# Batch 0's states fetched first, expert products begun during attention 1, and the side work of an expert stream dealt into other slots

## The chip, the core and the metric

The kernel runs on one core of one Trainium2 chip. The metric is device time in microseconds (us) of one execution; the time before is the median of three runs. The profile and its trace come from one further execution. Engines: PE (TensorE, matrix products; PEld is its weight load), DVE (VectorE), ACT (ScalarE), POOL (GpSimd) and SP (SyncE, which here only issues DMAs and reads expert numbers into registers).

## What is computed

A block of cross attention between tokens and a few state rows, then a mixture of experts with one expert per token:

```python
B, H, S, Ns, D = (8, 8, 512, 32, 64)
scores = scale * x @ state^T;  a  = softmax(scores);   xread = a @ state
scores2 = scale * state @ x^T; a2 = softmax(scores2);  sread = a2 @ x
x = concat([xread, sread], axis=2), heads joined      # 4352 rows of 512
logits = x @ w_gate                                    # 8 experts
e = argmax(logits); g = softmax(logits)[e]
out = g * (relu(x @ w1[e]) @ w2[e])                    # w1 512x1024, w2 1024x512
```

All of it is float32.

## The kernel before

**Token rows.** Of each batch the kernel finds the expert that most of its 512 tokens chose, and runs the whole batch through that expert. `load_w1(b, e)` and `load_w2(b, e)` fetch 2 MB each (w1 has one buffer, w2 two); `states_w1` multiplies the batch's states into w1 (tile G, through PSUM tile pG), `up` makes the hidden layer from the attention weights and G (PSUM tile ph, relu by ACT into hT), `down` the result (PSUM tile py, scaled by ACT into y and stored by ACT's DMA queue). The few token rows that chose otherwise are counted at the end (`left`) and redone in a branch.

**State rows.** The 256 rows of `sread` go to DRAM (`write_rows`), are read back, routed (`logits_s`), sorted by expert (`sort_states`) and run in `rounds`: three rounds of 128 rows, in each four groups of 32 rows with an expert of their own. A round streams 16 tiles of 1 MB (tile s, four DMAs of 256 KB each, three buffers for w1 and three for w2) through SP's queue: four steps of `round_up` (PSUM pgh), relu, transposes (`round_h`, PSUM pth), four steps of two `round_down` (PSUM pgy).

**Attention.** `front(b)`: DVE transposes x (xt) and the states (stT), PE makes the scores of both directions in the PSUM tile pa, DVE transposes them (sx) and takes maxima (mx, nm), ACT the exponentials (sx, and a for the second direction). `back(b)`: `turn_read` transposes the softmax (aT), `logits_x`, `route` and `choose` give the batch's expert number eb, `write_rows` transposes a (a2T) and makes the state rows.

**What sets the order.** Every engine runs its instructions in the order in which the program was written (class `InOrder`). `front`, `back`, `logits_s`, `sort_states` and `rounds` are generators: each `yield` ends a piece. `up` and `down` call `insert` twelve times for a batch, at every fourth product of 512 columns; each call advances the generator `others` by one piece, so that 96 slots of expert products take up the other work. `run(...)` advances a `front` and a `back` side by side, and a slot passes empty where both have ended. Fronts 0 to 2 and backs 0 and 1 lie ahead of the first slot, with DVE in POOL's place for two passes over sx (`early`).

**DMAs.** Those from SP and ACT share eight completion semaphores in turn, so that one may have to wait for an earlier one to land before it is issued; a DMA that waits holds up what stands behind it on the engine that issues it.

Of the kernel before, what the change touches and what calls it, by code (L numbers as in the profile page):

```python
# [20 lines left out]
def kernel(  # L21
# [70 lines left out]
    def load_x(b):  # L92
        x_nat[b] = att.tile([128, H, NC, D], FP32, tag="x", bufs=2, name="x_nat")
        for h in (slice(0, 4), slice(4, 8)):
            sp.dma_start(out=x_nat[b][:, h].rearrange("p h c d -> p h (c d)"),
                         in_=x[b, h].rearrange("h (p c) d -> p h (c d)", c=NC))
# [4 lines left out]
    def load_states(b0, b1):  # L101
        rows = state[b0:b1].rearrange("b h n d -> n (b h) d")
        for i in range(4):
            to = st4[ts(i, 32), b0 * H:b1 * H]
            if i % 2 == 0:
                act.dma_start(out=to, in_=rows)
            else:
                for u in range(2):
                    act.dma_start(out=to[:, :, ts(u, 32)], in_=rows[:, :, ts(1 - u, 32)])

    load_x(0)
    load_states(0, 1)
    load_x(1)


# [37 lines left out]
    wg = const.tile([128, NDC, E], FP32)  # L153
    act.dma_start(out=wg[:], in_=moe_w_gate.rearrange("(c p) e -> p c e", p=128))

# [12 lines left out]
    eb_f = const.tile([128, B, 1], FP32)  # L168
# [14 lines left out]
    load_states(1, B)  # L183
# [4 lines left out]
    blank = att.tile([128, XW], I32)  # L188
# [10 lines left out]
    def front(b, early):  # L199

        xt = att.tile([128, H, NC, 2, 32], FP32, tag="xt", name="xt")
        flat = "p h c d -> p (h c d)"
        for h in (slice(0, 4), slice(4, 8)):
            if h.start == 4:
                dve.transpose(stT[:, b].rearrange("p h u n -> p (h u n)"),
                              st4[:, ts(b, H)].rearrange("p h d -> p (h d)"))
            dve.transpose(xt[:, h].rearrange("p h c u t -> p (h c u t)"), x_nat[b][:, h].rearrange(flat))
            yield
# [13 lines left out]
        act.copy(gst[:, b, :, 0:E], pa[:, 2:4, 1, 0:E])  # L222
# [9 lines left out]
        if early:  # L232
            act.activation(sx[:], sx[:], AF.Exp, bias=0.0, scale=SCALE)
# [4 lines left out]
        yield  # L238
# [6 lines left out]
        if not early:  # L245
            act.activation(sx[:], sx[:], AF.Exp, bias=0.0, scale=SCALE)
            yield
# [5 lines left out]
        dve.tensor_scalar(s2[:], s2[:], 1e-9, None, ALU.add)  # L253
        dve.reciprocal(s2[:], s2[:])
# [3 lines left out]
    def write_rows(b):  # L258
# [7 lines left out]
        yield  # L266
# [6 lines left out]
        xs = att.tile([128, 2, D], FP32, tag="xs", bufs=2, name="xs")  # L273
# [4 lines left out]
        if b + 2 < B:  # L278
            load_x(b + 2)
# [4 lines left out]
    def logits_x(b):  # L284
# [5 lines left out]
        dve.transpose(lg[:, ts(b, NC)].rearrange("p c e -> p (c e)"), pl)  # L290

    def back(b, early):

        if early:
            turn_read(b)
            logits_x(b)
            route(lg[:, ts(b, NC), 0:E], b * NC, NC)
            choose(b, 1)
            yield
            yield from write_rows(b)  # L300
            yield
        else:
            w = write_rows(b)
            next(w)
            yield
            turn_read(b)
            for _ in w:
                pass
            yield
            logits_x(b)  # L310
            b0, nb = {B - 3: (0, 0), B - 2: (0, 0), B - 1: (B - 3, 3)}.get(b, (b, 1))
            if nb:
                route(lg[:, b0 * NC:(b0 + nb) * NC, 0:E], b0 * NC, nb * NC)
                yield
                choose(b0, nb)
            yield

    def logits_s():
# [3 lines left out]
        for _ in range(3):  # L322
            yield
        sT = att.tile([128, NST, NDC, 128], FP32, tag="sT", name="sT")
# [11 lines left out]
        route(lgs[:], NX, NST)  # L336
        yield

    def route(lg, u0, U):
# [16 lines left out]
        dve.tensor_reduce(gw[:, r, 0], ex[:], AX.X, ALU.add)  # L356
        dve.tensor_scalar(gw[:, r], gw[:, r], 1e-9, None, ALU.add)
        dve.reciprocal(gw[:, r], gw[:, r])

    def choose(b0, nb):  # L360

        pr = pa[:, 2, 1, 128:128 + nb * E].rearrange("p (b e) -> p b e", b=nb)
        ohb = oh[:, 0:NX].rearrange("p (b c) e -> p b c e", c=NC)
        for c in range(NC):
            pe.matmul(pr, lhsT=ones_b[:], rhs=ohb[:, ds(b0, nb), c, :],
                             start=(c == 0), stop=(c == NC - 1), skip_group_check=True)
        r = ds(b0, nb)
        dve.tensor_copy(out=cnt[:, r], in_=pr)
        dve.tensor_reduce(cmx[:, r, 0], cnt[:, r], AX.X, ALU.max)
        cc = att.tile([128, nb, E], FP32, tag="c_cc", bufs=1, name="c_cc")  # L370
        dve.tensor_tensor(cc[:], cnt[:, r], cmx[:, r].to_broadcast([128, nb, E]), ALU.is_ge)
        dve.tensor_tensor(cc[:], cc[:], rev8[:].unsqueeze(1).to_broadcast([128, nb, E]), ALU.mult)
        dve.tensor_reduce(eb_f[:, r, 0], cc[:], AX.X, ALU.max)
        dve.tensor_scalar(eb_f[:, r], eb_f[:, r], -1.0, float(E), ALU.mult, ALU.add)
        dve.tensor_copy(out=eb[:, r], in_=eb_f[:, r, 0])
# [62 lines left out]
    def down(hT, w2t, store, insert=None):  # L438
        for c in range(NC):
# [7 lines left out]
            if insert:  # L447
                insert()

# [99 lines left out]
    def round_x(r):  # L549
        pt = late["ps_t"].tile([128, NDC, 128], FP32, tag="t", name="ptx")  # L550
# [14 lines left out]
    def round_h(r):  # L565
        h = late["sst"].tile([128, F], FP32, tag="sh", bufs=1, name="sh")
        for half in range(2):
            relu(h[:, ts(half, 512)], rd[r]["ph"][half][:])
        hT = late["sst"].tile([128, NFC, 128], FP32, tag="shT", bufs=1, name="shT")
        for u in range(2):  # L570
            pt = late["ps_t"].tile([128, 4, 128], FP32, tag="t", name="pth")
# [30 lines left out]
    def rounds(r0, r1):  # L602
# [4 lines left out]
        for _ in range(3):  # L607
            yield
        for r in range(r0, r1):
# [4 lines left out]
            for k in range(NDC):  # L614
# [3 lines left out]
                if k % 2:  # L618
                    yield
            round_h(r)  # L620
            yield
            for f in range(0, NFC, 2):
# [4 lines left out]
                if f % 4:  # L627
# [4 lines left out]
    for _ in front(0, True):  # L632
        pass
    for _ in run(front(1, True), back(0, True)):
        pass
# [3 lines left out]
    for _ in run(front(2, True), back(1, True)):  # L639
        pass  # L640
# [14 lines left out]
    def batch(b):  # L655

        nonlocal G, hT
        if b + 1 < B:
            G = states_w1(w1s[b + 1], stT[:, b + 1])
            if 0 < b and b + 2 < B:  # L660
                load_w1(b + 2, expert_of(eb, b + 2))
        down(hT, w2s[b], store_batch(b), piece)
        if b + 2 < B:
            e = expert_of(eb, b + 2)
            if b == 0:
                load_w1(b + 2, e)
# [129 lines left out]
```

## Time and profile before

| | |
|---|---|
| time before, median of 3 runs (lowest to highest) | 606.71 us (602.52 to 609.12) |
| profiled execution, its own time / span of the trace | 607.1 us / 605.3 us |
| busy PE / DVE / ACT / POOL | 490.0 / 134.2 / 108.8 / 26.3 us |
| granted TensorE clock, mean | 0.958 of full speed |
| moved by DMA | 107.33 MB, mean 177 GB/s |
| first product of an expert (pG, then ph) | at 79.6 and 83.2 us |
| chain that ended last, by engine | PE 69%, DMA 12%, DVE 8%, ACT 4%, ACT's queue 3% |

Busy time of PE is that of pipelined matmuls whose ends are modelled. The chain that ended last is followed back from the last instruction; its shares say what the span was spent on. "idle before <-releaser" behind a row is the time for which the engine stood idle just before, and what ended it.

### The profile page before, as it was taken

To read this page: it belongs to the slowest core of one execution; us is meant where nothing else is said; L and a number is where in the kernel's file an instruction comes from. 1 tells how busy PE (TensorE), PEld (TensorE's weight loads), DVE (VectorE), ACT (ScalarE), POOL (GpSimd) and SP (SyncE) were. 2 spreads that over 40 slices of the span, in tenths; PEclk is the share of its full clock that TensorE was granted. 3 is DMA by queue.
4 is the path that set the end of the run, shared out by engine and by line. 5 is a ranking of instruction groups with operands and counts; after the bars stand their busy time and mean duration, and the time that the engine had idled before them with its cause. 6 is when DMAs were issued, how large, how long until landed. Compare 5 with 4: busy or idle time off the path is not lost.

```text
span 605.3 us, 8328 instructions
## 1 busy us (share of the span) xinstructions
PE 490.0 (81%) x3353; PEld 209.1 (35%) x3353; DVE 134.2 (22%) x312; ACT 108.8 (18%) x197; POOL 26.3 (4%) x30
## 2 busy tenths in 40 slices
PE   1131487895978979799999498999998999989996
PEld 0021333342433434344444033334233333333442
DVE  3366674505345043322030000000000000000000
ACT  0111141312213123221321022100211022011200
POOL 1000001101111011110010000000000000000000
PEclk9999979997978989799999799999998999999999
DMA  9918453320423214042448996887995999219100
GB/s 203 146 56 294 142 188 103 139 98 31 156 75 140 86 42 161 2 156 75 156 169 283 360 339 239 303 272 240 338 340 205 297 369 314 96 67 305 37 35 37
DMA packets 69532, 107.33 MB, mean 177 GB/s; under 512 B 17903, under 2 KB 27119, under 8 KB 69488
## 3 DMA queue, kind: packets, MB, share of 16 engines
q1 hardware_dynamic: 50896, 94.13, 45.8%
q10 hardware_dynamic: 18192, 11.56, 7.4%
q0 software_dynamic: 400, 1.05, 0.4%
q8 instruction: 28, 0.46, 0.3%
q14 instruction: 16, 0.13, 0.1%
HBM read 95.70 MB, written 11.28 MB: 177 GB/s over the span
## 4 chain that ended last, share of the span: by engine, by line
PE 69%; DMA 12%; DVE 8%; ACT 4%; ACTq 3%; SPq 2%; issue 2%; POOL 0%; POOLq 0%; DVEq 0%
PE py L48 33%; PE ph L48 17%; PE pa L48 8%; DMA s<-in_moe_w_dram 7%; PE pgy L48 4%; PE pG L48 3%; PE pgh L48 3%; ACTq L48 3%; DVE sx L48 3%; DMA out_dram<-y 2%; SPq L48 2%; DVE mx L48 2%; DVE nm L48 1%; DMA st<-in_state_dram 1%; ACT a2T L48 1%
## 5 line engine op out<-in xcount | busy, mean ns | idle before, releaser
L48 PE MATMUL py<-w2t,hT 128*128 128x512 f32 x512 | 233.7, 608 | 0.0
L48 PEld LDWEIGHTS py<-w2t,hT 128*128 128x128 f32 x512 | 96.1, 194 | 128.2 <-issue 120.7
L48 PE MATMUL ph<-aT,G 128*128 128x512 f32 x256 | 122.4, 627 | 0.0
L48 PEld LDWEIGHTS ph<-aT,G 128*128 128x128 f32 x256 | 49.4, 200 | 65.8 <-issue 62.4
L48 ACT ACTIVATE y<-py,gw 128x512 f32<-128x512 f32 x32 | 22.0, 687 | 234.4 <-PE py L48 225.7
L48 ACT ACTIVATE hT<-ph 128x512 f32<-128x512 f32 x64 | 38.2, 597 | 115.2 <-PE ph L48 115.2
L48 PE MATMUL pa<-aT,gst 128*32 128x128 f32 x128 | 7.4, 369 | 49.0 <-DVE aT L48 28.0
L48 PE MATMUL pgh<-s,sxT 128*32 128x512 f32 x192 | 36.0, 620 | 11.0 <-DMA s<-in_moe_w_dram 10.9
L48 PE MATMUL pgy<-s,shT 128*32 128x512 f32 x192 | 29.3, 600 | 0.8 <-DMA s<-in_moe_w_dram 0.8
L48 DVE COPY G<-pG 128x512 f32<-128x512 f32 x16 | 10.8, 687 | 65.1 <-PE pG L48 65.0
L48 DVE COPY shT<-pth 128x512 f32<-128x512 f32 x3 | 2.1, 691 | 92.6 <-PE pth L48 92.6
L48 PEld LDWEIGHTS pa<-aT,gst 128*32 128x32 f32 x128 | 4.4, 138 | 51.7 <-issue 51.6
L48 DVE STREAM_TRANSPOSE sx<-pa 128x256 f32<-128x256 f32 x32 | 11.5, 417 | 45.3 <-ACT gst L48 45.3
L48 DVE TENSOR_SCALAR ys<-pgy,xg 128x512 f32<-128x512 f32 x3 | 2.3, 751 | 83.7 <-PE pgy L48 83.7
L48 DVE STREAM_TRANSPOSE xt<-x_nat 128x1024 f32<-128x1024 f32 x16 | 19.5, 1218 | 5.2 <-DMA x_nat<-in_x_dram 5.2
L48 PEld LDWEIGHTS pgh<-s,sxT 128*32 128x32 f32 x192 | 6.9, 110 | 37.5 <-DMA s<-in_moe_w_dram 23.1
L48 PE MATMUL pa<-x_nat,a2T 128*32 128x64 f32 x512 | 10.5, 244 | 10.9 <-ACT sx L48 10.9
L48 PE MATMUL pG<-w1t,stT 64*32 64x512 f32 x256 | 18.9, 706 | 0.0
L48 PE MATMUL pa<-xt,stT 32*32 32x128 f32 x1024 | 18.5, 329 | 0.2 <-DVE xt L48 0.2
L48 POOL TENSOR_TENSOR sx<-sx,mx 128x1024 f32<-128x1024 f32 x5 | 9.6, 1911 | 179.0 <-DVE mx L48 179.0
L48 PE MATMUL pa<-ident,a 128*128 128x128 f32 x64 | 12.0, 318 | 6.2 <-ACT a2T L48 5.6
L48 DVE TENSOR_SCALAR xs<-pa,s 128x64 f32<-128x64 f32 x16 | 3.8, 280 | 55.1 <-ACT hT L48 20.3
(109 smaller groups left out, 226.5 us busy)
## 6 DMA issues: line engine op xcount, KB each, us to landing
s<-in_moe_w_dram SPq DMA_DIRECT2D x192, 256.0 KB, 5.2
w1t<-in_moe_w_dram SPq DMA_DIRECT2D x8, 2048.0 KB, 10.3
w2t<-in_moe_w_dram SPq DMA_DIRECT2D x8, 2048.0 KB, 9.7
x_nat<-in_x_dram SPq DMA_DIRECT2D x16, 512.0 KB, 3.5
out_dram<-y ACTq DMA_DIRECT2D x32, 256.0 KB, 4.8
ss_dram<-blank ACTq DMA_DIRECT2D x4, 257.0 KB, 4.6
st<-in_state_dram ACTq DMA_DIRECT2D x2, 448.0 KB
st<-in_state_dram ACTq DMA_DIRECT2D x4, 224.0 KB, 6.9
```

What stands on the lines that cost most here:

```text
L48: ins = getattr(self.engine, name)(*args, **kw)
```

## The change

At the start batch 0's states and the gate weights come ahead of x of batch 1 on ACT's queue, the states of the other batches and the blank rows go to SP's queue, and an Exp of one element loads ACT's table. `front` copies gst after the transposes of sx and not ahead of them; ends a piece after the maxima of sx, and takes nm and both exponentials in the next. `back` turns both softmaxes first, does the state rows and logits together, leaves a piece free, then chooses. Expert number 0 is read before front 1's scores; backs from batch 1 on and fronts from 2 on are in slots. `G` and `load_w1` for the next batches move from the head of a batch to the second and third row block of `down`. `rounds` waits five pieces for its first tiles (three before), its relu has a piece of its own, two of its free pieces go, and its transposes have two PSUM buffers. `choose` needs three steps to the number where it needed seven.

```diff
-    load_x(0)
-    load_states(0, 1)
-    load_x(1)
+    load_x(0, sp)
+    load_states(0, 1, act)
+    wg = const.tile([128, NDC, E], FP32)
+    act.dma_start(out=wg[:], in_=moe_w_gate.rearrange("(c p) e -> p c e", p=128))
+    load_x(1, act)
+    load_states(1, B, sp)
+    warm = const.tile([128, 1], FP32)
+    dve.memset(warm[:], 0.0)
+    act.activation(warm[:], warm[:], AF.Exp)
...
     for r in range(NR):
-        act.dma_start(out=ss_dram[ts(r, 128)], in_=blank[:])
+        sp.dma_start(out=ss_dram[ts(r, 128)], in_=blank[:])
...
-        act.copy(gst[:, b, :, 0:E], pa[:, 2:4, 1, 0:E])
...
             dve.transpose(sx[:, ts(i, 8)].rearrange("p b n -> p (b n)"), pc[:, i])
+        act.copy(gst[:, b, :, 0:E], pa[:, 2:4, 1, 0:E])
...
         eng.tensor_tensor(sx[:], sx[:], mx[:].to_broadcast([128, NB, NS]), ALU.subtract)
-        if early:
-            act.activation(sx[:], sx[:], AF.Exp, bias=0.0, scale=SCALE)
+        yield
+        act.activation(sx[:], sx[:], AF.Exp, bias=0.0, scale=SCALE)
...
-    def back(b, early):
...
+    def back(b):
+
+        turn_read(b)
+        turn_write(b)
+        yield
+        write_rows(b)
+        gates = logits_x(b)
+        yield
+        yield
+        choose(b)
+        if b == 1:
+            e1 = expert_of(eb, 1)
+            load_w1(1, e1)
+            load_w2(1, e1)
+        gates()
+        yield
...
-        for _ in range(3):
+        for _ in range(5):
             yield
...
-                if k % 2:
+                if k == 1:
                     yield
+            round_relu(r)
+            yield
             round_h(r)
             yield
...
-                if f % 4:
+                if f == 2:
                     yield
...
-    for _ in front(0, True):
+    one, two = front(0, True), front(1, True)
+    for _ in one:
         pass
-    for _ in run(front(1, True), back(0, True)):
-        pass
+    turn_read(0)
+    next(two)
+    gates = logits_x(0)
+    choose(0)
     e0 = expert_of(eb, 0)
     load_w1(0, e0)
     load_w2(0, e0)
-    for _ in run(front(2, True), back(1, True)):
-        pass
-    load_w2(1, expert_of(eb, 1))
+    next(two)
+    next(two)
+    turn_write(0)
+    next(two)
+    write_rows(0)
+    gates()
+    next(two)
...
-        for b in range(2, B):
-            yield from run(*([front(b + 1, False)] if b + 1 < B else []), back(b, False))
+        for b in range(1, B):
+            yield from run(back(b), *([front(b + 1, False)] if b + 1 < B else []))
...
+        def between(c):
+            nonlocal G
+            if c == 1 and b + 1 < B:
+                G = states_w1(w1s[b + 1], stT[:, b + 1])
+            if c == 2 and b + 2 < B:
+                load_w1(b + 2, expert_of(eb, b + 2))
+
+        down(hT, w2s[b], store_batch(b), piece, between)
```

`turn_write` is the first half of the old `write_rows` (transposes and copies of a2T) with the reciprocal of s that `front` had; `gates` is the end of the old `route`; `round_relu` the head of the old `round_h`.

ACT at the very start, before: st_77 are the states (32x8 rows are batch 0, 32x56 the other seven), wg the gate weights, blank the empty rows of the sorted states.

```order
L48 DMA st_77<-in_state_dram 32x8x32 x2
L48 DMA wg<-in_moe_w_gate_dram 128x4x8
L48 DMA st_77<-in_state_dram 32x56x64
L48 DMA st_77<-in_state_dram 32x56x32 x2
L48 DMA st_77<-in_state_dram 32x56x64
L48 DMA st_77<-in_state_dram 32x56x32 x2
L48 DMA ss_dram<-blank 128x514 x4
L48 ACT_TABLE_LOAD
L48 COPY gst<-pa 128x2x8
L48 ACTIVATE sx<-sx 128x1024
```

The same place of ACT in the changed kernel:

```order
L48 DMA st_77<-in_state_dram 32x8x32 x2
L48 DMA wg<-in_moe_w_gate_dram 128x4x8
L48 DMA x_nat<-in_x_dram 128x4x256 x2
L48 ACT_TABLE_LOAD
L48 ACTIVATE warm<-warm 128x1
L48 COPY gst<-pa 128x2x8
L48 ACTIVATE sx<-sx 128x1024
```

Ten DMAs have left the place ahead of the copy of gst, and two of x of batch 1 stand there.

PE ahead of the first expert product and just behind it, before (from the scores of front 2, the third of three):

```order
L48 MATMUL pa<-wg,stT 32x8 x8
L48 MATMUL pa<-xt,stT 32x128 x64
L48 MATMUL pa<-x_nat,a2T 32x64 x32
L48 MATMUL pG<-w1t,stT 32x512 x16
L48 MATMUL ph<-aT,G 128x512 x4
L48 MATMUL pa<-ident,a_627 128x128 x8
L48 MATMUL ph<-aT,G 128x512 x4
L48 MATMUL pa<-x_nat,a2T 32x64 x32
L48 MATMUL ph<-aT,G 128x512 x4
L48 MATMUL pa<-wg,stT 32x8 x8
L48 MATMUL pa<-xt,stT 32x128 x64
L48 MATMUL pa<-aT,gst 32x128 x8
```

PE in the changed kernel, from the scores of front 1, the second of two:

```order
L48 MATMUL pa<-xt,stT 32x128 x64
L48 MATMUL pa<-ident,a_244 128x128 x8
L48 MATMUL pa<-x_nat,a2T 32x64 x32
L48 MATMUL pG<-w1t,stT 32x512 x16
L48 MATMUL ph<-aT,G 128x512 x4
L48 MATMUL pa<-ident,a_392 128x128 x8
L48 MATMUL ph<-aT,G 128x512 x4
L48 MATMUL pa<-x_nat,a2T 32x64 x32
L48 MATMUL pa<-aT,gst 32x128 x8
L48 MATMUL ph<-aT,G 128x512 x4
L48 MATMUL pa<-wg,stT 32x8 x8
L48 MATMUL pa<-xt,stT 32x128 x64
```

One attention batch fewer stands ahead of pG, and in the slots the logits (aT,gst) have moved from behind the next front's scores (xt,stT) to a place ahead of them, with four products of ph between.

## Rows read from the trace of the kernel before

**Rows 1.** Windows: stretch, busy us (instructions) by engine, clock, DMA share, GB/s.

```profile
0.00:25.40 25.40, 3.61 (x144) 2.45 (x144) 4.91 (x14) 1.46 (x2) 2.09 (x15) 1.00 1.09 194
...
83.20:300.00 216.80, 184.15 (x1684) 87.01 (x1676) 74.90 (x170) 50.66 (x96) 19.11 (x10) 0.93 0.32 112
...
407.00:487.00 80.00, 75.57 (x287) 27.41 (x284) 3.52 (x5) 11.05 (x18) 0.98 (x1) 0.98 0.85 287
```

**Rows 2.** Timeline of the start: start us, us, engine, operation, idle before and releaser.

```profile
0.76 5.39 ACTq L48 DMA_DIRECT2D st<-in_state_dram  x6
...
7.55 13.52 ACTq L48 DMA_DIRECT2D st<-in_state_dram  x6
...
12.60 0.71 DVE L48 STREAM_TRANSPOSE stT<-st 128x512 f32<-128x512 f32 x1 [5.78 <-DMA wg<-in_moe_w_gate_dram]
...
14.49 2.68 PE L48 MATMUL pa<-xt,stT 32*32 32x128 f32 x112 [0.20 <-DVE xt L48]
...
25.16 0.17 ACT L48 COPY gst<-pa 128x16 f32<-128x16 f32 x1
25.37 1.44 DVE L48 STREAM_TRANSPOSE sx<-pa 128x256 f32<-128x256 f32 x4 [10.93 <-ACT gst L48]
```

**Rows 3.** Instructions on the states' tile st: time from issue to landing.

```profile
DMA to landing us min/median/max: 4.5/6.3/6.9
```

**Rows 4.** Timeline, from batch 0's softmax to the first expert products.

```profile
34.99 1.20 DVE L48 STREAM_TRANSPOSE aT<-sx 128x1024 f32<-128x1024 f32 x1
...
37.48 0.32 DVE L48 STREAM_TRANSPOSE lg<-pa 128x128 f32<-128x128 f32 x1 [1.29 <-PE pa L48]
...
40.58 0.15 DVE L48 CAST eb<-eb_f 128x1 int32<-128x1 f32 x1
...
41.45 0.39 SPq L48 DMA_DIRECT2D w1t<-in_moe_w_dram  x1
...
53.70 0.48 DVE L48 TENSOR_SCALAR xs<-pa,s 128x64 f32<-128x64 f32 x2 [1.89 <-PE pa L48]
...
55.94 1.23 DVE L48 TENSOR_TENSOR sx<-sx,sm 128x1024 f32<-128x1024 f32 x1
...
83.17 3.81 PE L48 MATMUL ph<-aT,G 128*128 128x512 f32 x8
```

**Rows 5.** The page: a costly group (busy us, mean ns), a DMA's issues (KB, us to landing).

```profile
L48 PE MATMUL pa<-x_nat,a2T 128*32 128x64 f32 x512 | 10.5, 244 | 10.9 <-ACT sx L48 10.9
...
w1t<-in_moe_w_dram SPq DMA_DIRECT2D x8, 2048.0 KB, 10.3
```

**Rows 6.** Timeline of PE in the expert stream, one attention batch, and its end four batches later.

```profile
88.14 0.66 PE L48 MATMUL pa<-ident,a 128*128 128x128 f32 x4 [0.73 <-ACT a2T L48]
...
93.19 3.70 PE L48 MATMUL ph<-aT,G 128*128 128x512 f32 x8
...
97.03 1.90 PE L48 MATMUL pa<-xt,stT 32*32 32x128 f32 x128
103.15 0.75 PE L48 MATMUL pa<-aT,gst 128*32 128x128 f32 x16 [4.21 <-DVE nm L48]
103.83 5.24 PE L48 MATMUL ph<-aT,G 128*128 128x512 f32 x8
...
248.96 6.05 PE L48 MATMUL ph<-aT,G 128*128 128x512 f32 x8
```

**Rows 7.** Waits from 84 to 300 us: engine, for whom, total us, times, longest us.

```profile
PE pa L48 <- DVE nm L48: 21.1, 5, 4.2
...
PE pa L48 <- ACT a L48: 6.7, 3, 2.6
```

**Rows 8.** Waits from 300 to 606 us, the same columns.

```profile
PEld pgh L48 <- DMA s<-in_moe_w_dram: 23.1, 17, 8.6
...
PEld pgy L48 <- DMA s<-in_moe_w_dram: 6.9, 10, 1.5
...
PE pth L48 <- ACT sh L48: 4.8, 3, 1.8
```

More of the change, by code (lines that the diff above doesn't have):

```diff
@@ L180, in evict @@
             dve.tensor_copy(out=dst, in_=src)
-    load_states(1, B)
     gst = att.tile([128, B, 2, 32], FP32, name="gst")
     dve.memset(gst[:], 0.0)
-    blank = att.tile([128, XW], I32)
+    blank = att.tile([128, XW], I32, tag="a2T", name="blank")
     gp.memset(blank[:], 0)
@@ L199, in front, with turn_x @@
     def front(b, early):
[L201 to L208, printed above, removed]
+        xt = att.tile([128, H, NC, 2, 32], FP32, tag="xt", bufs=2, name="xt")
+        def turn_x(h):
+            dve.transpose(xt[:, h].rearrange("p h c u t -> p (h c u t)"),
+                          x_nat[b][:, h].rearrange("p h c d -> p (h c d)"))
+        turn_x(slice(0, 4))
+        yield
+        turn_x(slice(4, 8))
+        dve.transpose(stT[:, b].rearrange("p h u n -> p (h u n)"),
+                      st4[:, ts(b, H)].rearrange("p h d -> p (h d)"))
+        yield
         for q in range(4):
@@ L265, in write_rows @@
             act.copy(a2T[:, g].rearrange("p (k c) r -> p k (c r)", k=2), pa[:, ts(g, 2), 1, :])
-        yield
+        dve.tensor_scalar(s2[:], s2[:], 1e-9, None, ALU.add)
+        dve.reciprocal(s2[:], s2[:])
+        soft[b] += (a2T,)
+    def write_rows(b):
+        _, _, s2, a2T = soft[b]
         pw = pa[:, 0, 1, 0:128].rearrange("p (g d) -> p g d", g=2)
@@ L290, in logits_x @@
         dve.transpose(lg[:, ts(b, NC)].rearrange("p c e -> p (c e)"), pl)
-    def back(b, early):
[L294 to L307, printed above, removed]
-                pass
[L309 to L316, printed above, removed]
+        return route(lg[:, ts(b, NC), 0:E], b * NC, NC)
+    def back(b):
[5 more added lines that the diff above has]
+        yield
+        yield
+        choose(b)
[4 more added lines that the diff above has]
+        gates()
+        yield
     def logits_s():
@@ L321, in logits_s @@
             sp.dma_start(out=srow[:, t, 0:DM], in_=st_dram[ts(t, 128)])
-        for _ in range(3):
+        for _ in range(4):
             yield
-        sT = att.tile([128, NST, NDC, 128], FP32, tag="sT", name="sT")
+        sT = att.tile([128, NST, NDC, 128], FP32, tag="sx", bufs=2, name="sT")
         pl = pa[:, 0, 0, 0:NST * E].rearrange("p (t e) -> p t e", t=NST)
@@ L335, in logits_s @@
         dve.tensor_copy(out=lgs[:], in_=pl)
[L336 removed]
+        gates = route(lgs[:], NX, NST)
+        yield
+        gates()
         yield
@@ L355, in route, with gates, choose @@
         act.activation(ex[:], sh[:], AF.Exp)
[L356 to L363, printed above, removed]
-        for c in range(NC):
[L365 to L375, printed above, removed]
+        def gates():
+            dve.tensor_reduce(gw[:, r, 0], ex[:], AX.X, ALU.add)
+            dve.tensor_scalar(gw[:, r], gw[:, r], 1e-9, None, ALU.add)
+            dve.reciprocal(gw[:, r], gw[:, r])
+        return gates
+    def choose(b):
+        pr = pa[:, 2, 1, 128:128 + E]
+        for c in range(NC):
+            pe.matmul(pr, lhsT=ones_b[:], rhs=oh[:, NC * b + c, :],
+                      start=(c == 0), stop=(c == NC - 1), skip_group_check=True)
+        dve.tensor_reduce(cmx[:, b], pr, AX.X, ALU.max)
+        cc = att.tile([128, E], FP32, tag="c_cc", bufs=2, name="c_cc")
+        dve.scalar_tensor_tensor(cc[:], pr, cmx[:, b], io8[:], ALU.is_ge, ALU.mult)
+        dve.tensor_reduce(eb[:, b:b + 1], cc[:], AX.X, ALU.max)
+        dve.tensor_copy(out=cnt[:, b], in_=pr)
     def expert_of(table, i, engines=(SP,)):
@@ L436, in up, with down @@
         return hT
-    def down(hT, w2t, store, insert=None):
+    def down(hT, w2t, store, insert=None, between=None):
         for c in range(NC):
@@ L448, in down @@
                 insert()
+            if between:
+                between(c)
     def store_batch(b):
@@ L549, in round_x @@
     def round_x(r):
-        pt = late["ps_t"].tile([128, NDC, 128], FP32, tag="t", name="ptx")
+        pt = late["ps_t"].tile([128, NDC, 128], FP32, tag="t", bufs=2, name="ptx")
         for c in range(NDC):
```

51 lines of the change are left out of this document (19 added, 32 removed).

## The prediction

> **What bounds the kernel now.** I read the page's slices first, then windows by stage, then the timeline of the two stretches in which PE does little, then the waits. In the first 25.4 us PE is busy for 3.6 [rows 1], and nothing of the experts' hidden layers runs before 83.17 us [rows 4], since the first expert number, and with it the first 2 MB of w1, comes late, and two batches' attention stands ahead. From 83 us to the end PE is the bound and nearly full, but it loses time in two places. From 83 to 300 us, where attention batches lie in the slots, it is idle for 216.8 - 184.2 = 32.6 us and its clock is 0.93 [rows 1]; the trace names two waits there, for nm and for a [rows 7]. From 300 us on, in the rounds, its products and still more its weight loads wait for streamed tiles [rows 8], while DMA moves 287 GB/s at a share of 0.85 [rows 1]. So the span is a start of 83 us, about 520 us of a PE stream, and a short tail. The change touches all three: it shortens the start, and deals the side work differently.
>
> **The start (term A).** Batch 0's scores are done at 14.49 + 2.68 = 17.17 us, but DVE may turn them only after ACT's copy of gst, and ACT stands in its DMA queue until 21.1 us and longer, behind the other batches' states and the blank rows: gst is copied at 25.16, sx begins at 25.37 [rows 2]. After the change ACT has x of batch 1 and the table ahead of it, and sx no longer waits for gst. When do batch 0's states land? Their last DMA was issued by 0.76 + 5.39 = 6.15; with the quickest landing of 4.5 us [rows 3] stT could start at 10.7, and before it started at 12.60 [rows 2]. x of batch 1 has left the competition, the other states have joined it; I take the middle, 11.6, and keep both ends. From stT to the end of the scores it was 17.17 - 12.60 = 4.6 us; xt now stands ahead of stT, so the 0.65 us in which PE waited for it inside goes: 3.9 us, and sx starts at 15.6, that is 9.8 us earlier. From sx to the end of aT it was 36.19 - 25.37 = 10.8 us [rows 2, 4], less one transpose of x (1.2 us) and the reciprocal pair of s (0.3 us) that stood between and now stand behind: 9.3 us, aT ends at 24.9. The first half of x of batch 1 (1.2 us on DVE) lies under PE's logits, as lg waited 1.3 us there [rows 4]. From aT's end to eb's end it was 40.73 - 36.19 = 4.5 us; four of seven steps at about 0.2 us each go, as do gw's three, which lay under PE's count: 3.8 us, eb at 28.7, and SP issues w1 0.7 us later as before [rows 4], at 29.4. It lands 10.3 us after that [rows 5], at 39.7.
>
> What PE and DVE must still do ahead of the first expert product is front 1 and back 0's state rows. Before, from eb's end to xs it was 53.70 - 40.73 = 13.0 us and to the end of the product of sx 57.17 - 40.73 = 16.4 us [rows 4]; this holds the same transposes of x and states, the same scores, maxima, exponentials and state rows. So the state rows end at about 41.7, w1 is there, PE makes pG, and DVE finishes sx at 45.1 plus 0.6 us for the gates; its first copy of G (0.7 us) follows. ph starts at about 46 with PE's state rows waiting for the exponential as before; without that wait I get 45. I take 45.7 instead of 83.17: **A = -37.5 us**, from -33 (states at 12.6, w1 landing 3 us later) to -40.
>
> By the Trainium skill (DMA: Bandwidth & Descriptors, section "Issuing engines are not separate DMA queues") DMAs from different engines' queues end up on the same 16 DMA engines and interleave, so that spreading them saves only the time to issue them. That speaks against the swap of queues: batch 0's states would land no sooner, stT would stay at 12.6, and the forecast would be 1.0 us higher; the gain from clearing ACT's queue would stay. The share of 1.09 over the first 25 us [rows 1] agrees that the engines were full there.
>
> **Work that moves (term B).** Back 1 and front 2 leave the start and enter the slots, where PE is the bound. Each attention batch costs PE there 1.8 us for the transposes with their inner wait (from the end of ph, 86.98, to 88.80 [rows 4, 6]), 10.5 / 8 = 1.3 us at most for state rows [rows 5], 0.7 us for logits, and 2.0 us for a front's scores (from the end of ph, 96.89, to 98.93) [rows 6]; the count is a few tenths: **B = +6 us**. Their DVE, ACT and POOL work is hidden by expert products, since DVE is busy for 75 of 217 us there [rows 1].
>
> **Waits in the slots (term C).** Before, logits_x stood directly behind the next front's scores in the same slot, so PE waited for DVE's whole pass over pa, up to nm: 4.2 us, five times, 21.1 us; three times choose waited for the exponentials of a, 6.7 us [rows 7]. Each such pause was followed by a slow stretch: the eight products behind it took 5.24 us, in the last of five 6.05, where they take 3.70 else [rows 6]; over the five the excess is 10.2 us, and with one pG and the logits at the lower clock about 12. After the change logits stand ahead of the scores; behind the scores comes a slot of products (3.5 us), and only then choose, which needs the four transposes of sx (1.4 us) and gst to be over. nm and both exponentials come after it, and PE meets pa next three slots (10 us) later: nm needs about 2.7 us after that point (four small steps, gates, nm), a 1.4 us more. So the waits go: **C = -40 us**; at worst half of it stays (-20).
>
> **New waits in the slots (term D).** The trace before has no row for the new order. Lower bound nothing; upper bound 2.0 us a batch, the size of the smaller waits in [rows 7], for seven batches, 14 us. The likeliest place: ACT is in order, and where the exponentials (1.1 + 1.4 us) and a y stand ahead of the copies of a2T, PE's second four transposes are late by about 1 us; stT may be late by a few tenths. The first ph also runs at the lower clock for some us. **D = +7 us.**
>
> **Rounds (term E).** Relu gets a slot of its own and the transposes a second buffer, so PE's waits around pth, 4.8 us for sh [rows 8] and about 2.4 for shT, go, but for 1 us: -6 us. The tiles: the queue of weight loads stood 23.1 + 6.9 = 30 us for them [rows 8]; since some of that passes while products still run, I count 25 us on the path. Two more slots (7 us) now lie between the first fetch and the first use, where the longest stall is (8.6 us), and load_w1 no longer stands at the head of a batch, where SP had to wait for pG with tiles queued behind. Against that, a round is 13 slots where it was 14. In the stretch of rounds PE has about 205 us of work (44 slots of 3.5 us, 50 us of round products, three pG), and DMA must move 50 MB of tiles, 8 MB of expert weights and 4 MB of results, 62 MB: 216 us at 287 GB/s [rows 1]. The two are nearly equal, so I let 20 of the 25 us stand. **E = -11 us**, from -25 to +25.
>
> **The sum.** 605.3 - 37.5 + 6 - 40 + 7 - 11 = 529.8 us of span; the profiled execution's own time is 607.1, so 1.8 us lie around it, which gives 531.6; the median of the runs shown is 0.4 below that execution: **531 us**.
>
> **Rivals.**
> - *The waits only change place* (12%). If PE waits at choose, or at the transposes, for DVE's pass as it did at logits, six fronts lose 8 us each: 531 + 48 - 7 = about 572. For it: pa is one tile of four banks, and its readers and writers waited for each other across parts. Against: a slot of products lies between.
> - *The rounds take the gain back* (14%). The stream starts at about 280 us, its bytes are the same, and at 250 GB/s, which is 287 less an eighth for buffers that stand full, 62 MB take 248 us where I allow 225: 531 + 23 = 554.
> - *The start does not do what it says* (6%). If SP's queue, with states and blanks ahead of w1, or batch 1's states hold the first expert back as before, A shrinks to about -10: 558. Against: the same bytes go in the same stretch, and before, ACT had issued the last of those states by 21.1 us [rows 2], 8 us ahead of the new issue of w1.
> - *Slower* (5%). SP's queue is in order and has three buffers per kind; if each of the 24 pairs of tiles stalls PE as the longest wait did (8.6 us [rows 8]), the rounds lose over 200 us. It decides at 531 + 82 = 613, so with the 20 us that I allow from 102 / 24 = 4.3 us a pair. Before, a pair cost 25 / 24 = 1.0 us.
>
> **Chances.** 63% for the forecast, whose own range is 510 to 548 (A to within 4, C down to -30, D 0 to 14, E -25 to +5). The range that should hold 8 in 10 takes in the rounds' rival at 554 and the start's at 558: 508 to 562. A measurement of this kernel, whose three runs span 1%, can tell about 1% from no change; all cases but the last are faster by more: 63 + 12 + 14 + 6 = 95%, of which I leave 2% within 1% for a larger loss in one of them; faster 93%, within 1% 2%, slower 5%.
>
> **What would show it.** In the profile after: gst copied behind sx, and sx starting near 15.6; w1's first issue near 29.4; ph from near 45.7; no wait of PE for nm, at most 2 us a batch between 46 and 240 us, and a clock near 1.0 there; in the rounds a total wait for tiles under 25 us, and pth without one. If ph starts after 52, A is wrong; if PE waits for nm or a in the slots, C; if PEld's wait for tiles exceeds 50 us, E.

## The result, and the profile after

| | before | after |
|---|---|---|
| time, median (lowest to highest) | 607.91 us (602.52 to 611.77) | 526.82 us (526.12 to 527.16) |
| span of the profiled execution | 605.3 us | 525.2 us |
| granted TensorE clock, mean | 0.958 | 0.994 |
| first product of an expert's hidden layer (ph) | 83.2 us | 48.1 us |

The ratio of after to before is 0.869, with a 95% interval of 0.863 to 0.875: 81 us less, where 76 were forecast (531 us, range 508 to 562). The page has PE busy for 467.5 us instead of 490.0: its ph products take 600 ns on the mean instead of 627, at the higher clock of the table.

The timeline of the start after the change, its columns as in [rows 2] (start us, us, engine, operation, idle before and releaser):

```profile
12.13 0.71 DVE L48 STREAM_TRANSPOSE stT<-st 128x512 f32<-128x512 f32 x1 [2.82 <-DMA st<-in_state_dram]
...
16.01 1.44 DVE L48 STREAM_TRANSPOSE sx<-pa 128x256 f32<-128x256 f32 x4 [3.17 <-PE pa L48]
...
17.55 0.17 ACT L48 COPY gst<-pa 128x16 f32<-128x16 f32 x1 [7.32 <-DVE sx L48]
...
29.31 0.16 DVE L48 TENSOR_REDUCE eb<-c_cc 128x1 int32<-128x8 f32 x1
...
30.18 0.40 SPq L48 DMA_DIRECT2D w1t<-in_moe_w_dram  x1
...
39.81 1.22 DVE L48 TENSOR_REDUCE nm<-pa 128x2 f32<-128x1024 f32 x1 [1.13 <-ACT a2T L48]
...
42.83 1.93 PE L48 MATMUL pa<-x_nat,a2T 128*32 128x64 f32 x64 [3.67 <-ACT a L48]
44.69 3.48 PE L48 MATMUL pG<-w1t,stT 64*32 64x512 f32 x32
...
48.10 1.13 PE L48 MATMUL ph<-aT,G 128*128 128x512 f32 x2
```

sx starts as soon as PE's scores are done, and gst stands behind it. What answers to [rows 4]: eb at 29.31 instead of 40.58, w1's issue at 30.18 instead of 41.45, ph at 48.10 instead of 83.17. One wait has another end: PE's state rows, the third row from the end, stand 3.67 us for ACT's exponentials of a, where before the change they stood 5.44 us for that of sx (twice, the 10.9 us of [rows 5]).

Windows after the change, columns as in [rows 1]; the first two hold the attention batches in the slots, the others the rounds:

```profile
45.00:150.00 105.00, 99.28 (x1116) 47.32 (x1104) 51.49 (x122) 30.60 (x58) 11.47 (x6) 1.00 0.43 148
150.00:265.00 115.00, 109.50 (x947) 52.17 (x943) 38.98 (x101) 31.26 (x58) 11.47 (x6) 1.00 0.37 129
265.00:360.00 95.00, 92.90 (x337) 36.97 (x336) 6.41 (x31) 17.21 (x29) 2.13 (x2) 1.00 0.88 298
360.00:430.00 70.00, 64.48 (x250) 23.03 (x249) 3.52 (x5) 10.15 (x17) 0.98 (x1) 0.95 0.89 302
```

In the slots PE is idle for 220 - 208.8 = 11.2 us, where it was 32.6 of 216.8 [rows 1], and the clock is 1.00 where it was 0.93. PE's waits from 45 to 265 us, columns as in [rows 7]:

```profile
PE pa L48 <- ACT a2T L48: 4.9, 7, 0.7
...
PE pa L48 <- DVE xs L48: 4.6, 7, 0.7
...
PE pa L48 <- ACT sT L48: 1.4, 1, 1.4
```

Neither nm nor a is among them. From 265 us on, what answers to [rows 8] is:

```profile
PEld pgh L48 <- DMA s<-in_moe_w_dram: 18.9, 16, 6.0
...
PE pgh L48 <- DMA s<-in_moe_w_dram: 8.1, 5, 5.1
...
PEld pgy L48 <- DMA s<-in_moe_w_dram: 5.0, 11, 1.2
```

PE's wait of pth for sh is gone; the wait for tiles is smaller, not gone.

### The profile page after: what moved, and what is told of

It reads as the page before. It is cut to its first block, busy times and chain, and to the rows that moved or that the text cites. A ratio compares the mean times of both kernels' runs of the same rounds, so it can differ in the third digit from the quotient of the medians.

```text
span 525.2 us, 8352 instructions
## 1 busy us (share of the span) xinstructions
PE 467.5 (89%) x3361; PEld 201.3 (38%) x3361; DVE 129.0 (25%) x317; ACT 110.3 (21%) x200; POOL 30.1 (6%) x32
## 5 line engine op out<-in xcount | busy, mean ns | idle before, releaser
L48 PE MATMUL py<-w2t,hT 128*128 128x512 f32 x512 | 229.8, 599 | 0.0
L48 PEld LDWEIGHTS py<-w2t,hT 128*128 128x128 f32 x512 | 94.0, 190 | 122.7 <-issue 111.2
L48 PE MATMUL ph<-aT,G 128*128 128x512 f32 x256 | 116.3, 600 | 0.3 <-DVE G L48 0.3
L48 PEld LDWEIGHTS ph<-aT,G 128*128 128x128 f32 x256 | 47.1, 191 | 60.7 <-issue 57.4
L48 PE MATMUL pgh<-s,sxT 128*32 128x512 f32 x192 | 34.4, 619 | 8.2 <-DMA s<-in_moe_w_dram 8.1
L48 POOL TENSOR_TENSOR sx<-sx,mx 128x1024 f32<-128x1024 f32 x6 | 11.5, 1912 | 171.7 <-DVE mx L48 171.7
L48 PEld LDWEIGHTS pgh<-s,sxT 128*32 128x32 f32 x192 | 6.9, 110 | 33.1 <-DMA s<-in_moe_w_dram 18.9
L48 PE MATMUL pa<-aT,gst 128*32 128x128 f32 x128 | 5.6, 296 | 14.3 <-DVE aT L48 9.7
L48 DVE STREAM_TRANSPOSE sx<-pa 128x256 f32<-128x256 f32 x32 | 11.5, 417 | 23.2 <-PE pa L48 23.2
L48 PE MATMUL pG<-w1t,stT 64*32 64x512 f32 x256 | 17.1, 647 | 0.0
L48 POOL DMA_INDIRECT out_dram<-ys,xg x3 | 2.9, 981 | 229.9 <-DMA s<-in_moe_w_dram 164.7
L48 PE MATMUL pa<-wg,stT 64*32 64x8 f32 x128 | 2.3, 189 | 15.5 <-DVE stT L48 15.5
```

The source lines that it names most:

```text
L48: ins = getattr(self.engine, name)(*args, **kw)
```

## The experiments

Each edits the changed kernel, or the kernel before where it says so. The times of before beside them had medians of 604.6 (e1 to e4), 607.2 (e5, e6, e7, e9) and 605.8 us (e8, e10 to e12); ratios are to these, with 95% intervals. Two ratios of this study whose intervals overlap widely are called not told apart.

### The start: queues and the place of gst

`e1_old_queues` puts the DMAs back on their old queues, with gst behind sx as after the change:

```diff
-    load_x(1, act)
-    load_states(1, B, sp)
+    load_x(1, sp)
+    load_states(1, B, act)
...
-        sp.dma_start(out=ss_dram[ts(r, 128)], in_=blank[:])
+        act.dma_start(out=ss_dram[ts(r, 128)], in_=blank[:])
```

> The changed kernel with the DMAs of the start on the queues that they had before: x of batch 1 on SP, the other batches' states and the blank rows on ACT. gst stays behind the transposes of sx. Theory (ACT's queue held the start back): ACT stands in its queue until about 24 us, so the copy of gst and the exponential of sx come at about 25 instead of 17.6 and 20.0; sx itself still starts at 16; ph 5 us later, time 532. Rival A (the queues don't matter, all DMAs share the engines): 527. Rival B (the swap brought batch 0's states earlier and that is the gain): stT later by several us, time 537.

`e2_gst_first` leaves the queues as changed and copies gst ahead of the transposes of sx:

```diff
+        act.copy(gst[:, b, :, 0:E], pa[:, 2:4, 1, 0:E])
         for i in range(4):
             dve.transpose(sx[:, ts(i, 8)].rearrange("p b n -> p (b n)"), pc[:, i])
-        act.copy(gst[:, b, :, 0:E], pa[:, 2:4, 1, 0:E])
```

> The changed kernel with the copy of gst ahead of the transposes of sx, as before, in the start and in the slots. Theory: with ACT free the place of gst costs 0.2 us in the start and some tenths a batch, 527 to 529. Rival (that gst stood ahead of sx was itself the 10 us of the start): 537.

`e10_old_start` makes both edits together.

> The changed kernel with both parts of its start's order undone together: the queues as before the change, and gst copied ahead of the transposes of sx as before it. Apart, the first put w1's issue at 33.95 us instead of 30.18 and the second left it where it was (29.73). Theory (gst ahead of sx costs nothing only while ACT is free; with the states and blank rows on ACT's queue ACT comes to gst at about 23.4 us, and sx, the routing of batch 0 and w1 wait behind it, as before the change): sx near 23.9 us instead of 16.0, w1's issue near 38, the first ph near 55, and 526.8 + 7.5 = 532 to 537 us. Rival (what the start loses is given back where the rounds wait for their transfers, as the old queues alone suggest): the start is as late, and the time 524 to 529 us.

Measured: e1 525.34 us (ratio 0.869, 0.861 to 0.876), e2 523.98 (0.864, 0.857 to 0.871), e10 532.34 (0.876, 0.871 to 0.881). In e1 w1 is issued at 33.95 us and ph starts at 51.49, 3.4 later than after the change, but no loss of time can be measured: the theory's 532 us is missed, and rival A's 527 is nearer. Where the late start is made up for is not shown. In e1's trace the stretch behind the sort of the state rows is 7.3 us shorter than after the change, but e8's, whose start is on time, is as short (243.9 and 244.3 us against 251.2). In e2 gst is copied at 15.34, w1 issued at 29.73 and ph started at 47.84: the place of gst costs nothing there. Both together give what neither gives alone. The timeline of e10:

```profile
7.63 12.99 ACTq L48 DMA_DIRECT2D st<-in_state_dram  x6
...
12.01 0.71 DVE L48 STREAM_TRANSPOSE stT<-st 128x512 f32<-128x512 f32 x1 [3.85 <-DMA wg<-in_moe_w_gate_dram]
...
23.45 0.17 ACT L48 COPY gst<-pa 128x16 f32<-128x16 f32 x1 [1.30 <-issue]
23.66 1.44 DVE L48 STREAM_TRANSPOSE sx<-pa 128x256 f32<-128x256 f32 x4 [10.94 <-ACT gst L48]
...
37.83 0.39 SPq L48 DMA_DIRECT2D w1t<-in_moe_w_dram  x1
```

ACT stands in the issue of six DMAs for 13 us, gst waits behind, and sx for gst, 7.7 us later than after the change; ph starts at 55.21, 7.1 later, and the median is 5.5 us higher. The theory holds, at its lower edge; since the intervals of the ratios still overlap a little, the trace carries it more than the time. The two edits remove one and the same wait: either is enough for most of it.

### The slots: what made PE wait for nm and a

`e3_two_ahead` does batch 1's routing and front 2 ahead of the first slot, as before the change, and leaves six slots empty instead:

```diff
+    turn_read(1)
+    three = front(2, True)
+    next(three)
+    gates = logits_x(1)
+    choose(1)
...
```

> The changed kernel with back 1 and front 2 ahead of the first expert product, as before, and six slots left empty in their place. Theory (what stands ahead of the first product is latency, not PE work): the start grows by one batch's chain, about 24 to 26 us, and the slots lose 6 us of PE work: 545 to 548. Rival (the batch in the slots costs about what it cost ahead of them): 527 to 532.

540.9 us (0.891, 0.884 to 0.898). The first product of G, and the first of `sort_states`, which comes behind the attention batches:

```profile
69.37 3.67 PE L48 MATMUL pG<-w1t,stT 64*32 64x512 f32 x32
...
291.89 0.17 PE L48 MATMUL pa<-oh,U 128*128 128x8 bf16 x1
```

pG starts at 69.37 instead of 44.69, so 24.7 us later, and 14.1 us of that stay in the time. From the first ph (72.96) to the sort it takes 218.9 us; after the change it takes 225.9 (48.10 to 274.00), with the same 392 expert products. So the moved work costs 7.0 us in the slots, its waits included, as terms B and D have it for this batch and front (6 and 1). The rival (the slots cost all of it) is out. The theory's time is 4 to 7 us too high all the same: 24.7 - 7.0 is 17.7 us, and the times differ by 14.1. The spans of the two traces differ by 16.7, and e3's four times by 4.6, so that this rest is within the spread of single executions.

`e4_logits_nm` keeps the change's start and rounds and deals the slots' pieces as before: logits right behind the next front's scores, nm in the piece of sx, and the softmax of sx turned a piece behind that of a:

```diff
-        yield
-        act.activation(sx[:], sx[:], AF.Exp, bias=0.0, scale=SCALE)
...
+        yield
+        act.activation(sx[:], sx[:], AF.Exp, bias=0.0, scale=SCALE)
...
-        gates = logits_x(b)
         yield
+        gates = logits_x(b)
...
-            yield from run(back(b), *([front(b + 1, False)] if b + 1 < B else []))
+            yield from run(*([front(b + 1, False)] if b + 1 < B else []), back(b))
```

> The changed kernel with the old order in the slots: the logits directly behind the next front's scores, nm in the same piece as sx. Theory (PE waits at the logits for DVE's pass over pa): six waits of 4.2 us come back, with the exponentials' wait at choose and a slow clock behind each, about 6 us more a batch for some: 27 to 45 us, 554 to 572. Rival (the start's shortening gave the gain, and waits hide in the slots): under 535.

589.0 us (0.971, 0.965 to 0.978): the order of the pieces alone takes back 62 of the 81 us, more than expected. It is lost in the slots: from the first ph to the sort the trace takes 285.6 us instead of 225.9. Waits of PE from 48 to 270 us, and two windows:

```profile
PE pa L48 <- DVE nm L48: 23.5, 6, 3.9
...
PE pa L48 <- ACT a L48: 16.1, 5, 3.6
```

```profile
48.00:150.00 102.00, 81.50 (x887) 38.56 (x872) 44.37 (x91) 23.25 (x45) 9.56 (x5) 0.93 0.40 138
150.00:270.00 120.00, 96.64 (x918) 45.27 (x917) 45.54 (x97) 23.42 (x46) 11.47 (x6) 0.86 0.25 86
```

The waits are the old ones of [rows 7], and now nearly every batch has both. PE is idle for 43.9 us of 222, and the clock falls to 0.86 in the second window. The eight products behind a pause show it:

```profile
70.24 0.64 PE L48 MATMUL pa<-aT,gst 128*32 128x128 f32 x16 [3.92 <-DVE nm L48]
70.81 5.40 PE L48 MATMUL ph<-aT,G 128*128 128x512 f32 x8
```

They take 5.40 us where eight take 3.6 to 3.7 elsewhere in this trace.

`e5_own_psum_before` asks why PE has to wait at all. It is the kernel before, in its old order; two results get PSUM tiles of their own instead of a corner of pa:

```diff
-        pl = pa[:, 1, 1, 0:128]
+        pl = ps_p.tile([128, 512], FP32, tag="p", name="pl")[:, 0:128]
...
-        pr = pa[:, 2, 1, 128:128 + nb * E].rearrange("p (b e) -> p b e", b=nb)
+        pr = ps_p.tile([128, 512], FP32, tag="p", name="pr")[:, 0:nb * E].rearrange("p (b e) -> p b e", b=nb)
```

> The kernel before, with the order of its work untouched; only the logits' result pl and choose's row pr leave the PSUM tile pa for tiles of their own out of the pool of the expert products. Theory (term C: what the slots lose before the change is that PE's logits and choose stand in a tile that DVE and ACT are still at, 5 waits of 4.2 us for nm and 3 of 6.7 us for ACT's a, and the slow products behind them): these waits go, and most of the 40 us of C with them: 565 to 580 us. Rival (the waits are set by the order alone: the logits need something that DVE makes only behind nm, so another tile changes nothing): 600 to 608 us.

576.02 us (0.946, 0.938 to 0.953), 31 us less than before by two lines, and the theory's range holds it. Its first ph is at 82.03 us, where before it was at 83.17 [rows 4], and from there to the sort it takes 198.3 us instead of 228.0, so the gain is in the slots. There, as in [rows 1] and [rows 6]:

```profile
83.00:300.00 217.00, 204.23 (x1807) 97.61 (x1806) 78.93 (x196) 55.28 (x105) 21.25 (x12) 0.98 0.40 139
```

```profile
97.83 0.64 PE L48 MATMUL pl<-aT,gst 128*32 128x128 f32 x16
98.41 3.70 PE L48 MATMUL ph<-aT,G 128*128 128x512 f32 x8
```

The logits, in the same place of the program, no longer wait, and the eight products behind them take 3.70 us instead of 5.24 [rows 6]. The logits' operands were there all the time; PE waited since DVE was still reading the scores, in other parts of the tile into which the logits were to go. Choose no longer waits for a, but 4.3 us in two waits for its operand oh: that much is due to the order. The logits went into pa[:, 1], which also holds a quarter of the scores that nm reads; whether a quarter of pa without scores would have done, e5 does not tell.

### The waits that the change left

`e6_own_psum_after` does the like for the changed kernel, for the logits' result and the state rows':

```diff
-        pw = pa[:, 0, 1, 0:128].rearrange("p (g d) -> p g d", g=2)
+        pw = ps_p.tile([128, 512], FP32, tag="p", name="pw")[:, 0:128].rearrange("p (g d) -> p g d", g=2)
...
-        pl = pa[:, 1, 1, 0:128]
+        pl = ps_p.tile([128, 512], FP32, tag="p", name="pl")[:, 0:128]
```

> The changed kernel, with the state rows' result pw and the logits' result pl in PSUM tiles of their own out of the pool of the expert products. Theory (the waits that the change left, 7 of 0.66 us for xs and 3.67 us for ACT's a at the start, come from sharing the tile pa): they go, 526.8 - 4.6 - 3.7 = 518.5, so 517 to 521 us. Rival 1 (what the slots gain is waited for again in the rounds, whose tiles come at the pace of the transfers): 524 to 527 us. Rival 2 (the two tiles more make the expert products wait for a free buffer): 527 to 535 us.

`e9_own_psum_G` besides moves the line `G = states_w1(w1s[0], stT[:, 0])` ahead of the last `next(two)`.

> The kernel with pw and pl in tiles of their own, and besides G of batch 0 put one step earlier in the program, ahead of the last piece of front 1, so that the copies out of pG are ahead of that piece's work on DVE and ACT. Theory (the start ends with a chain pG, its copies, ph; the copies wait behind front 1's): 1.5 to 3 us less than with the tiles alone, 515 to 519 us. Rival (w1 lands later than that, or the rounds wait for what is gained): within 1 us of the kernel with the tiles alone.

`e12_own_psum_a2` besides gives the second four transposes of a (g = 1) a tile of their own:

```diff
+        own = ps_p.tile([128, 512], FP32, tag="p", name="pt2")
+        pt = [pa[:, 0:2, 1, :], own[:].rearrange("p (k s) -> p k s", k=2)]
...
-                pe.transpose(pa[:, 2 * g + c // 2, 1, ts(c % 2, 128)], a2[:, g, c, :], ident[:])
+                pe.transpose(pt[g][:, c // 2, ts(c % 2, 128)], a2[:, g, c, :], ident[:])
...
```

> The kernel with pw and pl in tiles of their own and G one step earlier (515.1 us), and besides the second four transposes of a in a tile of their own, so that they need not wait for the copy of the first four out of pa (7 waits of 0.7 us in the slots and one at the start). Theory: these go, 515.1 - 4.9 - 0.7 = 509.5, so 508 to 512 us. Rival (the third tile of the pool of four that a batch takes makes the expert products wait, or the rounds wait for what is gained): 514 to 518 us.

Measured: e6 515.78 us (0.847, 0.841 to 0.852), e9 515.11 (0.845, 0.839 to 0.851), e12 507.79 (0.835, 0.830 to 0.839). e6 and e9 are not told apart: the place of G is worth less than expected or nothing, as e9's rival has it. The tiles are worth 11 and then 7 us, a little more than the waits that they remove and than was expected, and no loss in the rounds eats them up. No wait for xs is left in e6's slots, and none for a2T in e12's. Here the two sides were in different quarters of pa: the logits go into pa[:, 1] while xs reads pa[:, 0], the second four transposes into pa[:, 2:4] while the copy reads pa[:, 0:2]. So the waits that this program sets went by the whole tile. e12 is 19 us faster than the changed kernel, with the arithmetic untouched. Its timeline of the start, and its two windows of the slots:

```profile
37.73 1.93 PE L48 MATMUL pw<-x_nat,a2T 128*32 128x64 f32 x64
...
41.92 3.67 PE L48 MATMUL ph<-aT,G 128*128 128x512 f32 x8
```

```profile
45.00:150.00 105.00, 104.48 (x1198) 51.95 (x1197) 55.59 (x133) 32.52 (x63) 15.29 (x8) 1.00 0.49 170
150.00:265.00 115.00, 113.61 (x877) 54.88 (x876) 35.12 (x109) 32.02 (x59) 9.78 (x6) 1.00 0.39 137
```

The state rows start 5.1 us earlier and ph 6.2 us earlier than after the change; PE's idle time from 45 to 265 us is 1.9 us instead of 11.2. That is 15.5 of the 18.8 us between the two spans (525.2 and 506.4).

### The rounds

`e7_old_rounds` cuts the rounds into pieces as before the change:

```diff
-        for _ in range(5):
+        for _ in range(3):
...
-                if k == 1:
+                if k % 2:
...
-            yield
             round_h(r)
...
-                if f == 2:
+                if f % 4:
```

and has one PSUM buffer for the transposes.

> The changed kernel with the rounds cut into pieces as before the change (three pieces of waiting for the first tiles, relu in the piece of a product, the old free pieces, one PSUM buffer for the transposes). Theory (term E: the gain of 15.5 us after the sort, forecast as 11, comes from these edits): 535 to 543 us. Rival (it comes from tiles that are fetched earlier for other reasons and from the clock; the pieces are worth the transposes' waits alone, 3 of 4.8 us at most): 526 to 532 us.

`e11_old_relu` takes back only relu's own piece and the second buffer; the waiting and the free pieces stay as changed.

> The changed kernel with relu of a round in the piece of its transposes and one PSUM buffer for these, as before the change; the five waiting pieces and the fewer free ones stay. It divides the 11.8 us that the rounds' old pieces cost all together. Theory (the transposes' waits for relu and for their one buffer, 4.1 and 2.5 us in the trace with all old pieces, are paid in full and PE's clock after them in part): 532 to 535 us, and the first tiles and free pieces hold the other half. Rival (the whole 11.8 us is the first tiles' wait of 7 to 8 us and the slow products behind it): 526 to 529 us.

Measured: e7 538.64 us (0.887, 0.882 to 0.892), e11 527.16 (0.868, 0.863 to 0.872). The pieces cost 11.8 us all together, and relu's piece with the second buffer has no part in it that can be measured: e11's theory (532 to 535 us) failed, its time is the rival's. PE's waits in the rounds of e11, from 265 us on:

```profile
PE pth L48 <- ACT sh L48: 3.5, 3, 1.2
...
PE pgh L48 <- DMA s<-in_moe_w_dram: 3.1, 2, 2.1
```

The wait for sh is back with 3.5 us, and that for tiles is 3.1 instead of 8.1. It would fit that what PE loses at the transposes it does not lose at the next tile, which has landed meanwhile. This is not shown: in the ten traces with the rounds as after the change PE's wait for these tiles is anything from 3.4 (e10) to 8.7 us (e2). In e7 the first tiles are late:

```profile
304.85 3.94 PE L48 MATMUL pgh<-s,sxT 128*32 128x512 f32 x8 [7.11 <-DMA s<-in_moe_w_dram]
308.72 4.76 PE L48 MATMUL py<-w2t,hT 128*128 128x512 f32 x8
```

From the first transposes of a round (ptx, at 287 us in e7 and 294 after the change) PE makes 148 matmuls in 43 us in e7 and 169 after the change, at a clock of 0.88 and 1.00. How much of the 11.5 us between e7 and e11 is the first wait and how much the free pieces was not tried apart.

### The place of G and load_w1

`e8_w1_head` makes G and issues w1 at the head of a batch again, from batch 1 on:

```diff
+        if 0 < b and b + 1 < B:
+            G = states_w1(w1s[b + 1], stT[:, b + 1])
+            if b + 2 < B:
+                load_w1(b + 2, expert_of(eb, b + 2))
...
-            if c == 1 and b + 1 < B:
+            if b == 0 and c == 1:
...
```

> The changed kernel with G and load_w1 of the next batches at the head of a batch again (from batch 1 on; for batch 0 as the change has them, since expert number 1 is not there yet). Theory (these products are the same in either place, the next w1 is there long before it is wanted, and what stands behind load_w1 on SP's queue has slack until the rounds): 525 to 529 us. Rival (G at the head makes PE wait for w1 or for its copies, or SP waits for PE's reads of w1 and holds up the loads behind it): 530 to 536 us, with PE waits of pG for w1t or of up for G.

524.39 us (0.864, 0.859 to 0.869): not told apart from the changed kernel. In its trace PE waits 2.8 us for copies of G, as the rival has it, and takes 4.0 us more from the first ph to the sort; behind the sort it takes 6.9 us less, which lies within the spread of that stretch. The new place is worth nothing by itself that can be measured.

## Why the prediction was right, and where its terms were off

The parts are read at three marks: the first ph; the first product of sort_states; the end. Between them I subtract the expert products, eight in 3.44 us as in these two rows of after, and 1.9 us for each pG; what is left is side work and stalls.

```profile
261.91 3.60 PE L48 MATMUL py<-w2t,hT 128*128 128x512 f32 x8
265.35 1.85 PE L48 MATMUL pa<-wg,sT 128*128 128x8 f32 x16
...
274.00 0.17 PE L48 MATMUL pa<-oh,U 128*128 128x8 bf16 x1
```

Before, that last product is at 311.19 us, behind 328 products of ph and py; after, at 274.00, behind 392.

| stretch | before | after | measured | forecast |
|---|---|---|---|---|
| to the first ph (A) | 83.2 | 48.1 | -35.1 | -37.5 |
| to the sort, less products and pG (B + C + D) | 228.0 - 148.5 = 79.5 | 225.9 - 176.1 = 49.8 | -29.7 | +6 - 40 + 7 = -27 |
| to the end, less products and pG (E) | 294.1 - 194.8 = 99.3 | 251.2 - 167.3 = 83.9 | -15.4 | -11 |

Together -80.2, and the spans differ by 80.1. Each trace is one execution: in the four with this start (after, e7, e8, e11) ph comes at 45.5 to 48.1 us, and the ten with these rounds take 243.9 to 251.9 us from the sort to the end (after the change 251.2). Taken back singly, the parts cost 14.1 (e3), 5.5 (e10), 62.2 (e4) and 11.8 us (e7), 93.6 together, so they overlap.

**A.** Of the 35 us, e3 gives 24.7 (at pG) to the batch and front that left the start, e10 7.1 to the queues and gst; the rest was not tried. The steps to w1 came as forecast: sx at 16.01 (15.6), w1 issued at 30.18 (29.4). The wait of 0.65 us for xt that the prediction takes off is that of the weight loads, PE itself stood for 0.20 [rows 2]; from stT to the end of the scores it took 3.8 us all the same, as forecast (3.9). The step "from eb's end to xs 13.0 us as before" was off: it took 15.4 (from 29.47 to 44.90 us). Before, the state rows stood in the program ahead of front 1's exponentials of a, and waited by the trace only for that of sx. The change put them behind these exponentials, which read pa, and their result went into pa too: they waited 3.67 us for them. It also put the transposes of a ahead of nm, which waited for ACT's copies out of pa (1.13 us in the row at 39.81). e6, with a tile of their own for the state rows, starts them 3.4 us earlier, and e12 5.1. From xs to ph it took 3.2 us where 4.0 were forecast, which hid a part of the miss.

By the rule that I weighed against the swap of queues (the Trainium skill, DMA: Bandwidth & Descriptors, section "Issuing engines are not separate DMA queues") the states would land no sooner. The runs agree as far as they can tell: stT starts at 11.44 to 12.49 us in ten traces with the queues swapped (12.13 after the change), and at 11.85 and 12.01 with the old ones in e1 and e10. I had taken 11.6. What the swap does is to keep ACT out of the issue of states and blank rows, and e1 shows that this matters little once sx does not wait for gst.

**B and C.** The prediction took the waits for nm and a, and the slow products behind them, for 40 us that the new order removes. No such wait is left, the clock is 1.00, and the old dealing brings them back (e4, with 62 us, since batch 1 and front 2 are now in the slots too and both waits come in nearly every batch). e5 shows the cause, which was only named in passing, in the first rival: the waits come from the shared tile. Without the sharing the old order costs 31 us less. The first rival, that the waits change place at 572 us, did not happen. The prediction's reason, the slot of products between, fits but was not tried by itself; the rival's mechanism is real all the same, as e4 shows at a still higher price.

**D.** Its size was about right (the new waits come to 4.6 us, and 7 were forecast), the place was not. I expected the second four transposes to come later than before; they wait 0.7 us a batch, as they did before [rows 6]. New are 0.7 us a batch of the logits for xs: state rows and logits, now in one slot, both go into pa. With tiles of their own this wait is gone (e6, e9, e12).

**E.** Transfers run at 298 to 302 GB/s from 265 to 430 us, more than the 287 of before [rows 1], so the rival by which the rounds take the gain back (554 us) did not come about, and the one that ends slower (4.3 us of waiting for each of 24 pairs of tiles) is far off: PE waits 8.1 us for all of w1's. The wait of the weight loads for tiles is 18.9 + 5.0 = 23.9 us, forecast under 25. The size of the term, -11, is what the rounds' pieces are worth (11.8 in e7), but its division failed: "-6 us for the waits around pth" was worth nothing that can be measured (e11), and the whole came from the pieces for the tiles. So it is partly luck that the size fits. I had added the two as if independent; while the transfers set the pace, a pause of PE at the transposes may be time in which the next tile lands, which is not shown. PE's work in the rounds was also added up wrongly, 154 + 50 + 6 = 210 us and not 205; the term does not hang on it. The other 4 us of the measured -15.4 have no experiment of their own and lie within the 8 us by which this stretch differs between traces; e8 shows no gain from the place of load_w1, which I had counted among the reasons.

## What to carry to other kernels

When an engine waits for another with its operands at hand, look at where its result goes: a wait for a reader of the same PSUM tile can be removed by another tile (two lines, 31 us in the kernel before) as well as by another order of the work (62 us after the change, where more batches have it), and what the order leaves the tiles still remove (19 us). Price a pause of PE with the products behind it, not by its own length. In a stretch that is held by transfers, do not add up the waits: here those at the transposes were worth nothing and the pieces ahead of and between the tiles all of it, so measure one before paying for the others.

## What the runs showed of the hardware that was not expected

- **A pause cost almost half its length again.** In e4 a wait of 3.92 us was followed by eight products in 5.40 us instead of 3.60 to 3.70; so were all six such waits for nm, in 5.40 to 6.16 us. Not every pause did this: behind waits of 2.97 and 3.59 us for a, at 79 and 117 us, 24 products took 10.54 and 16 took 7.11, as after the change (10.55 and 7.11); behind two others of 2.97 us 24 took 13.46 and 13.51. With both waits in nearly every batch the granted clock of a stretch of 120 us was 0.86, a mean over its two levels of 2.4 GHz (1.00) and 1.2 GHz; in e12, with PE idle for 1.9 us in 220, it was 1.00.
- **Issuing six DMAs held ACT for 13 us.** In e10 the issue of states runs from 7.63 to 20.62 us, and the table, the blank rows and gst come behind it.
- **Two edits that leave sx in its place apart move it by 7.7 us together.** sx starts at 15.72 us with the old queues, at 15.55 with gst ahead, at 23.66 with both, against 16.01.
